# Linear attention and an MLP on one core: first turns of a group moved ahead of the stores, two PSUM tiles moved to other banks, one sum moved to VectorE

## The chip, the cores and the metric

The kernel runs on one NeuronCore of a Trainium2 chip. The time is the device time of one execution in microseconds; the median of three runs before the change is 224.44 us (221.71 to 224.67).

## The reference

For each of 4 batches and 8 heads, 768 tokens of width 64 go through a causal linear attention with a decay `lam` per head, and the result, 3072 tokens of 512 values, through an MLP of 512 to 2048 to 512 whose activation is Mish:

```python
for b in range(nb):                                   # blocks of 64 tokens
    intra = einsum('bhic,bhjc->bhij', qb, kb) * Dmask[None]
    intra = einsum('bhij,bhjd->bhid', intra, vb)
    inter = einsum('bhid,bhde->bhie', qb * lam_pow[None], kv_state)
    out[:, :, sl] = intra + inter
    kv_state = lam_block * kv_state + einsum('bhsd,bhse->bhde', kb * rev_pow[None], vb)
h = x @ w_in                                          # (3072, 512) x (512, 2048)
g = h * tanh(log1p(exp(h)))
result = g @ w_out                                    # (3072, 2048) x (2048, 512)
```

## The kernel before

**Groups and rounds.** The 768 tokens of a batch are cut into 6 chunks of 128 (`C`). Group n is chunk n of all four batches: 512 tokens, 4 chunks numbered i = 4n + b. The outer loop over n ("round n") runs the MLP of group n and, in between, the attention of group n + 1. A round is a list of units for TensorE (PE): 16 units of the first layer (`mm1_unit`: 4 matmuls of 128x512 into a bank `ph`, then Mish on ScalarE into `hsg`), then for n >= 1 fourteen halves of the second layer (`fast_unit`: 7 products x, z, x, z, y, z, y for 2 token blocks, 8 matmuls of 128x256 each). The seven products are a Strassen-like scheme: `token_sum` makes sums `gsum` of Mish outputs on VectorE (DVE), and `after` combines the products (`p1`, `p7`, `u3`, `u2`, `osum`) and stores four quarters.

**Attention of groups 2 to 5** comes in pieces, of which `room` says how many are done after which unit. `chunk_a` forms k^T v (`pv`), adds the old state (`raw`, DVE), multiplies by the decay (`w`, GpSimd, which is POOL in the profile), and turns chunk b + 2. `chunk_s` forms the scores `pS` from the transposed k and q and masks them (`sb`, DVE). `chunk_o` forms the output `pO`, scales it (`xtok`, DVE) and transposes it by DMA into `xt`, which the first layer of the next round reads. The 12 pieces of a group stand as a, s, a, s, o, a, s, o, a, s, o, o. Groups 0 and 1 have other pieces (`first_*`, `att_*`).

**A turn** (`turn(i)`) scales k by its decay into `ktil` (POOL; DVE for the last group), then issues two DMA transposes on SP's queue: `qraw` from q and `kraw` from `ktil`. The scores of chunk i need both. The first two turns of a group were made at unit 0 of the round, the other two in `chunk_a` of chunks 0 and 1.

**Queues.** The order within each engine is the order in which the code is written. SP issues the transposes of `turn`, those of `xtok`, and the stores of `after` at steps 4, 5 and 6 (units 25, 27, 29); each waits for its source, and what stands behind it waits as well. POOL issues the loads of k, q and v (`later`: 12 for the group after next, spread over a round) between its own arithmetic.

**PSUM** has 8 banks: `ph` 2, `po` 2 (products x, z, y and unit 2 of the first layer), `pS`, `pk`, `pq` and `pO` one each. A tile whose name takes a bank waits until the readers of the tile before in that bank are done.

Of the kernel before, what the change touches and what calls it, by code (L numbers as in the profile page):

```python
# [7 lines left out]
F32 = mybir.dt.float32  # L8
# [12 lines left out]
def kernel(  # L21
# [10 lines left out]
    nc = tc.nc  # L32
    B, H, S, D = q.shape
    C = 128
    NG = S // C
    JP = H // 2
# [231 lines left out]
    def turn(i):  # L268

        scale_k(i)  # L270
        for src, name, to in ((qn, "qraw", qraw), (ktil, "kraw", kraw)):
            to[i] = work.tile([128, JP, C], F16, name=name, tag=name, bufs=4)
            nc.sync.dma_start_transpose(out=to[i], in_=src[i].rearrange("p h c -> p (h c)"))
# [103 lines left out]
    def chunk_a(s):  # L377

        n, b = s.n, s.b
        i = n * B + b  # L380
        if n < NG - 1:
            pv = ps.tile([128, JP, 128], F32, name="pv", tag="pq")
            for j in range(JP):
                nc.tensor.matmul(  # L384
                    pv[:, j, :].rearrange("p (a e) -> p a e", a=2),
                    ktil[i][:, 2 * j : 2 * j + 2, :].rearrange("p h c -> p (h c)"),
                    vz[i % NVB][:, 2 * j : 2 * j + 2, 0:D], start=True, stop=True,
                )
            for hf in range(2):
                raw = work.tile([128, 2, 128], F32, name="raw", tag="raw", bufs=3)  # L390
                hs = slice(2 * hf, 2 * hf + 2)
                nc.vector.tensor_tensor(  # L392
                    out=raw, in0=pv[:, hs, :], in1=wst[b][hf][n % 2], op=ALU.add)
                nc.gpsimd.tensor_tensor(  # L394
                    out=wst[b][hf][(n + 1) % 2], in0=raw, in1=lbm[:, hs, :], op=ALU.mult)
        if i + 2 < (n + 1) * B:
            turn(i + 2)
# [15 lines left out]
    def chunk_o(s):  # L413

        n, b = s.n, s.b
        i = n * B + b
        if xt[n] is None:
            xt[n] = work.tile([128, JP, GT], F16, name="xt", tag="xt", bufs=2)
        psO = ps.tile([128, H, D], F32, name="pO", tag="pO")
        for j in range(JP):  # L420
            nc.tensor.matmul(  # L421
                psO[:, 2 * j : 2 * j + 2, :].rearrange("p h e -> p (h e)"), qraw[i][:, j, :],
                wst[b][j // 2][n % 2][:, j % 2, :], start=True, stop=False)
            for t in range(2):
                nc.tensor.matmul(psO[:, 2 * j + t, :], s.sb[t][:, j, :],  # L425
                                 vz[i % NVB][:, 2 * j + t, 0:D], start=False, stop=(t == 1))
        xtok = work.tile([128, H, D], F16, name="xtok", tag="xtok", bufs=4)
        nc.vector.tensor_tensor(out=xtok, in0=psO, in1=bc(lqt, 2, D), op=ALU.mult)  # L428
        nc.sync.dma_start_transpose(
            out=xt[n][:, :, b * C : (b + 1) * C], in_=xtok.rearrange("p h e -> p (h e)"))  # L430
# [196 lines left out]
    def after(n, step):  # L627

        if step == 0:
            nc.scalar.activation(keep(n, "p1"), bank[n, "x", "all"], AF.Copy)  # L630
        elif step == 1:
            nc.scalar.activation(keep(n, "p7"), bank[n, "z", "all"], AF.Copy)
        elif step == 2:
            o = work.tile([128, 2, HN], F32, name="osum", tag="osb", bufs=4)
            nc.scalar.activation(o, bank[n, "x", "all"], AF.Copy)
            store(n, 0, 0, o, nc.scalar)
        elif step == 3:
            nc.vector.tensor_tensor(  # L638
                out=keep(n, "u3"), in0=bank[n, "z", "all"], in1=kept[n, "p1"], op=ALU.add)
            nc.gpsimd.tensor_tensor(  # L640
                out=keep(n, "u2"), in0=kept[n, "u3"], in1=kept[n, "p7"], op=ALU.subtract)
        elif step == 4 and n < NG - 1:
            plus(n, 1, 1, "y", kept[n, "u3"])
        elif step == 4:
            o = work.tile([128, 2, HN], F32, name="osum", tag="osb", bufs=4)
            for t, b, lo, w in bank[n, "y"]:
                nc.vector.tensor_tensor(out=o[:, b, lo : lo + w], in0=t,
                                        in1=kept[n, "u3"][:, b, lo : lo + w], op=ALU.add)
            store(n, 1, 1, o, nc.sync)
        elif step == 5:  # L650
            plus(n, 1, 0, "z", kept[n, "p1"])
        elif step == 6:
            plus(n, 0, 1, "y", kept[n, "u2"])
# [53 lines left out]
    for n in range(NG):  # L707
        units = [(mm1_unit, (n, ni)) for ni in range(NKI)]

        if n == 0:  # L710
            units += [(mm2_unit, (n, b2 + b, part)) for b2 in range(0, B, 2) for part in range(WS)
                      for b in range(2)]
        else:
            units += [(fast_unit, (n, step, blk)) for step in range(7) for blk in range(2)]
        pieces = []
        if n + 1 < NG:
            pieces = att_pieces(n + 1) if n + 1 < NT else chunk_pieces(n + 1)
        if n == 0:

            i = max(i for i, (f2, _) in enumerate(pieces) if f2 is att_a)  # L720
            pieces[i : i + 3] = pieces[i + 1 : i + 3] + pieces[i : i + 1]

        if n == 0:
            room = dict(zip(range(24, 32), (1, 2, 3, 3, 3, 3, 3, 3)))
        else:
            first = 8 if n == 1 else 5
            span = len(units) - 8 - first
            room = {first + u: (u + 1) * len(pieces) // span - u * len(pieces) // span
                    for u in range(span)}
        if n == 1:  # L730

            for ni in range(3):
                mm1_part(n, ni, 0, GT - C)
                while late and ni < 2:
                    f2, s = late.pop(0)
                    f2(s)
                    if f2 is att_o:
                        break
        later = []
        if 1 <= n < NG - 2:  # L740
            later = [(lambda f=f, i=i: f(i)) for i in range((n + 2) * B, (n + 3) * B)
                     for f in (load_k, load_q, load_v)]
        nl = len(later)
        for u, (fn, args) in enumerate(units):
            rest = fn(*args)
            while later and (nl - len(later)) * len(units) <= u * nl:
                later.pop(0)()
            if n == 0 and 19 <= u < 23:
                weight_sum(0 if u < 21 else 2, u % 2)
            if n == 1 and 4 <= u < 8:  # L750
                weight_sum(1 if u < 6 else 3, u % 2)
            if n > 0 and u in (9, 10):
                token_sum(n, 2, u - 9)
            if n > 0 and u == NKI - 3:
                token_sum(n, 0, 0)
            if n > 0 and u == NKI - 2:
                token_sum(n, 1, 0)
            if n > 0 and u == NKI - 1:
                token_sum(n, 0, 1)
                token_sum(n, 1, 1)  # L760
            if n > 0 and u in (NKI + 2, NKI + 3):
                token_sum(n, 3, u - NKI - 2)
            if n == 0 and 2 <= u < 2 + nh:
                att_kv(first_halves[u - 2], "po")
                att_w(first_halves[u - 2])
            if n == 0 and u % 2 == 1 and 0 < (u + 1) // 2 < B:
                scale_k((u + 1) // 2)
            if n == 0 and nh + 2 <= u < nh + 2 + NVB - B:
                nc.vector.memset(vz[u - nh - 2 + B][:, :, D : 2 * D], 0.0)
            if n == 0 and nh + 2 <= u < nh + 2 + NKB:  # L770
                nc.vector.memset(kz[u - nh - 2], 0.0)
            if n == 0 and u == 17:
                q_decays()
            if n == 0 and u == 16:
                nc.vector.tensor_scalar(out=maskT, in0=rel, scalar1=0.0, scalar2=None, op0=ALU.is_ge)
            if n == 0 and u == 18:
                scale_k(B)
            if n > 0 and pieces and u == 0:
                if n > 1:
                    turn((n + 1) * B)  # L780
                turn((n + 1) * B + 1)
            for _ in range(room.get(u, 0)):
                f2, s = pieces.pop(0)
                s.spare = "po" if u < NKI - 1 else "ph"
                f2(s)
            if n == 0 and rest:
                rest()
        if n == 0:
            late = pieces
            while ahead:  # L790
                ahead.pop(0)()
# [30 lines left out]
```

## Time and profile before

| | |
|---|---|
| profiled execution | 222.32 us |
| span of its instructions | 220.3 us |
| granted TensorE clock, mean | 0.991 |
| PE busy | 200.6 us (91%) |
| DVE busy | 123.0 us (56%) |
| POOL busy | 116.3 us (53%) |
| ACT busy | 90.3 us (41%) |
| moved by DMA | 26.75 MB, mean 121 GB/s |
| DMA transposes on SP | 48, median landing 3.1 to 4.3 us |

Busy time is the time in which an engine had an instruction running; PEld, the weight load, runs beside PE. An engine's idle time matters where the work that ends last waits for it. In the timelines a row gives start, time, engine, line, operation and out<-in; the brackets at the end hold the idle time of the engine before it and what ended that. Names in brackets such as kraw(10) mean the tile of chunk 10; in the rows the numbers are left out.

### The profile page before, as it was taken

Reading aid. Unit: us, or ns where it says so; the run is one execution under the profiler, and the core shown is the slowest. Engines: PE = TensorE matmul, PEld = TensorE weight load, DVE = VectorE, ACT = ScalarE, POOL = GpSimd, SP = SyncE. Lnnn points to the kernel's source line nnn. Section 1 sums busy time; section 2 is a strip of 40 time slices with the busy share of each in tenths; the row PEclk is TensorE's granted clock in tenths of the full one; section 3 lists DMA queues with packets and bytes.
Section 4 is the critical chain, followed back from the end, with each engine's and each line's share of the span. In section 5 each row is a group of like instructions: output and inputs, shape, how many; then the busy total and the mean of one; then the engine's idle time right before and its main releaser. Section 6 shows DMA issues by size and latency. Waiting matters only on the chain.

```text
span 220.3 us, 4222 instructions
## 1 busy us (share of the span) xinstructions
PE 200.6 (91%) x1672; PEld 129.0 (59%) x1672; DVE 123.0 (56%) x229; ACT 90.3 (41%) x159; POOL 116.3 (53%) x140
## 2 busy tenths in 40 slices
PE   7899999999993996996998993998999999999993
PEld 2465544676541686743587741576854587744893
DVE  6658653777543895315986302897345865313433
ACT  5565566667651321163431061532046531176410
POOL 7996335998999643956961955765600001100020
PEclk9999999999998899999999999999999999999999
DMA  9999999998999988899899799299596313310014
GB/s 128 149 153 201 205 205 169 182 136 125 147 145 149 135 74 119 115 195 132 88 94 143 95 188 164 35 122 88 122 191 128 71 27 95 107 39 0 1 54 140
DMA packets 112469, 26.75 MB, mean 121 GB/s; under 512 B 102594, under 2 KB 111938, under 8 KB 112450
## 3 DMA queue, kind: packets, MB, share of 16 engines
q0 software_dynamic: 78080, 13.37, 83.6%
q1 hardware_dynamic: 31392, 10.49, 25.0%
q10 hardware_dynamic: 2978, 2.62, 3.9%
q8 instruction: 13, 0.21, 0.4%
q14 instruction: 6, 0.05, 0.1%
HBM read 27.26 MB, written 6.29 MB: 152 GB/s over the span
## 4 chain that ended last, share of the span: by engine, by line
PE 71%; DMA 11%; DVE 8%; POOL 4%; issue 3%; SPq 1%; ACT 1%; ACTq 0%; DVEq 0%
PE ph L482 28%; PE z L587 12%; DMA kraw<-ktil 9%; PE y L587 6%; PE po L504 6%; PE x L587 5%; DVE gsum L560 2%; PE pS L406 2%; DVE sb L411 2%; DMA qn<-in_q_dram 2%; POOL kn L69 2%; PE fin L587 2%; PE pO L421 2%; PE pO L425 1%; PE pO L249 1%
## 5 line engine op out<-in xcount | busy, mean ns | idle before, releaser
L482 PE MATMUL ph<-xt,win 128*128 128x512 f16 (+2 forms) x404 | 90.5, 371 | 0.4 <-ACT hsg L496 0.2
L496 ACT ACTIVATE hsg<-ph 128x512 f16<-128x512 f32 x96 | 57.0, 597 | 79.0 <-PE ph L482 78.9
L482 PEld LDWEIGHTS <-win 128*128 128x128 f16 x404 | 36.8, 98 | 37.3 <-issue 1.4
L640 POOL TENSOR_TENSOR u<-u,p 128x512 f32<-128x512 f32 x5 | 6.3, 1263 | 63.8 <-DVE u L638 63.8
L587 PEld LDWEIGHTS <-gsum 128*128 128x128 f16 x336 | 31.2, 98 | 3.3
L394 POOL TENSOR_TENSOR w<-raw,lbm 128x256 f16<-128x256 f32 x24 | 19.2, 817 | 19.4 <-DVE raw L392 19.3
L411 DVE TENSOR_TENSOR sb<-pS,maskT 128x512 f16<-128x512 f32 x32 | 20.5, 680 | 13.9 <-PE pS L406 13.9
L587 PEld LDWEIGHTS <-hsg 128*128 128x128 f16 x240 | 22.6, 98 | 4.0
L69 POOL DMA_DIRECT2D kn<-in_k_dram x23 | 21.2, 923 | 4.7 <-DMA wout<-in_moe_w_out_dram 1.7
L77 POOL DMA_DIRECT2D qn<-in_q_dram x23 | 21.0, 913 | 4.8 <-DMA wout<-in_moe_w_out_dram 3.3
L560 DVE TENSOR_TENSOR gsum<-hsg 128x1024 f16<-128x1024 f16 x20 | 15.7, 785 | 13.5 <-ACT hsg L496 13.5
L80 POOL DMA_DIRECT2D vz<-in_v_dram x24 | 21.6, 903 | 3.0 <-DMA wout<-in_moe_w_out_dram 1.7
L587 PE MATMUL x<-wout,hsg 128*128 128x256 f16 x160 | 20.5, 273 | 0.0
L587 PE MATMUL z<-tsum,gsum 128*128 128x256 f16 x160 | 19.3, 273 | 0.0
L392 DVE TENSOR_TENSOR raw<-pv,w 128x256 f32<-128x256 f32 x24 | 9.1, 416 | 16.1 <-PE pv L384 15.5
L264 POOL TENSOR_TENSOR ktil<-kn,lk 128x512 f16<-128x512 f16 x15 | 15.8, 1063 | 0.1
L504 PE MATMUL po<-wout,hsg 128*128 128x512 f16 x64 | 15.1, 379 | 0.0
L406 PE MATMUL pS<-qraw,kraw 64*128 64x128 f16 x128 | 6.6, 224 | 8.7 <-DMA kraw<-ktil 8.7
L428 DVE TENSOR_TENSOR xtok<-pO,lqt 128x512 f16<-128x512 f32 x16 | 11.0, 685 | 5.1 <-PE pO L425 5.1
L421 PE MATMUL pO<-w,qraw 128*128 128x128 f16 x64 | 9.2, 223 | 4.0 <-DVE xtok L428 4.0
L406 PEld LDWEIGHTS <-kraw 64*128 64x128 f16 x128 | 3.7, 96 | 14.7 <-DMA kraw<-ktil 10.2
L425 PEld LDWEIGHTS <-sb 128*128 128x128 f16 x128 | 8.2, 100 | 4.7 <-issue 4.3
(101 smaller groups left out, 236.7 us busy)
## 6 DMA issues: line engine op xcount, KB each, us to landing
out_dram<-osum SPq DMA_DIRECT2D x14, 256.0 KB, 3.3
vz<-in_v_dram POOLq DMA_DIRECT2D x24, 128.0 KB, 5.5
kn<-in_k_dram POOLq DMA_DIRECT2D x23, 128.0 KB, 4.9
qn<-in_q_dram POOLq DMA_DIRECT2D x23, 128.0 KB, 4.8
wout<-in_moe_w_out_dram POOLq DMA_DIRECT2D x4, 512.0 KB, 16.1
win<-in_moe_w_in_dram POOLq DMA_DIRECT2D x3, 512.0 KB, 9.7
out_dram<-osum ACTq DMA_DIRECT2D x5, 256.0 KB, 3.0
out_dram<-osb ACTq DMA_DIRECT2D x4, 256.0 KB, 5.3
```

Source lines behind the costliest of these rows:

```text
L69: nc.gpsimd.dma_start(out=kn[i], in_=chunk_rows(k, i))
L77: nc.gpsimd.dma_start(out=qn[i], in_=chunk_rows(q, i))
L80: nc.gpsimd.dma_start(out=vz[i % NVB][:, :, 0:D], in_=chunk_rows(v, i))
L264: (nc.vector if i <= B or i >= (NG - 1) * B else nc.gpsimd).tensor_tensor(out=t, in0=kn[i], in1=bc(lk, 2, D), op=ALU.mult)
L394: nc.gpsimd.tensor_tensor(out=wst[b][hf][(n + 1) % 2], in0=raw, in1=lbm[:, hs, :], op=ALU.mult)
L406: nc.tensor.matmul(pS[t][:, j, :], kraw[i][rs, j, :], qraw[i][rs, j, :], start=True, stop=True)
L411: nc.vector.tensor_tensor(out=s.sb[t], in0=pS[t], in1=bc(maskT, 1, JP), op=ALU.mult)
L482: nc.tensor.matmul(ph_t[ni][:, lo:hi], win0[min(ni, 2)][:, kc, max(ni - 2, 0) * 128 : max(ni - 2, 0) * 128 + 128] if ni < w else win[ni // ...
L496: nc.scalar.activation(hsg[n][:, ni, :], ph_t.pop(ni), AF.Mish)
L504: nc.tensor.matmul(po, hsg[n][:, ki, b * C : (b + 1) * C], wout[part][:, kk, :], start=(ki == 0), stop=(ki == NKI - 1),)
L560: nc.vector.tensor_tensor(out=gsum[n, i][:, ks, :], in0=a, in1=b, op=op)
L587: nc.tensor.matmul(t, lhs(kk, b), rhs(kk, c, c + w), start=(fresh and kk == 0 and (alone or i == 0)), stop=(kk == HK - 1), skip_group_chec ...
```

## The change

Four things are named in its title, and the diff shows two more.

- For groups 3, 4 and 5 the first two turns are made after units 23 and 25 of the round before, and no longer at unit 0. Group 2 keeps its second turn at unit 0 of round 1.
- `pv` of the chunks takes a bank of `po` (up to unit 14) or of `ph` (from unit 15 on), and `pO` takes the banks `pO` and `pq` in turn.
- `u2 = u3 - p7` runs on DVE and no longer on POOL.
- In rounds 2 to 4 each attention piece comes two units earlier (`first` 3 where it was 5). Round 1 keeps its places.
- The 12 loads of a round start at unit 1 and end by unit 23, where they ran from unit 0 to unit 27.

```diff
-            pv = ps.tile([128, JP, 128], F32, name="pv", tag="pq")
+            pv = ps.tile([128, JP, 128], F32, name="pv", tag=s.spare, bufs=2)
...
-        psO = ps.tile([128, H, D], F32, name="pO", tag="pO")
+        psO = ps.tile([128, H, D], F32, name="pO", tag=("pO", "pq")[b % 2])
...
                 out=keep(n, "u3"), in0=bank[n, "z", "all"], in1=kept[n, "p1"], op=ALU.add)
-            nc.gpsimd.tensor_tensor(
+            nc.vector.tensor_tensor(
                 out=keep(n, "u2"), in0=kept[n, "u3"], in1=kept[n, "p7"], op=ALU.subtract)
...
-            first = 8 if n == 1 else 5
-            span = len(units) - 8 - first
+            first = 8 if n == 1 else 3
+            span = (22 if n == 1 else 20) - first
             room = {first + u: (u + 1) * len(pieces) // span - u * len(pieces) // span
                     for u in range(span)}
...
-            while later and (nl - len(later)) * len(units) <= u * nl:
+            while later and u >= 1 and (nl - len(later)) * 24 <= (u - 1) * nl:
                 later.pop(0)()
...
-            if n > 0 and pieces and u == 0:
-                if n > 1:
-                    turn((n + 1) * B)
+            if n == 1 and u == 0:
                 turn((n + 1) * B + 1)
+            if n > 0 and n + 2 < NG and u in (23, 25):
+                turn((n + 2) * B + (u - 23) // 2)
```

How this moves instructions shows at three places. On SP's queue at the end of round 1, from the last transposed output of group 2 on (`osum` rows are the stores of steps 4, 5 and 6); before:

```order
L429 DMA_TRANSPOSE xt_1107<-xtok_1300 128x4x128
L615 DMA out_0_dram<-osum_1342 128x2x256
L615 DMA out_0_dram<-osum_1363 128x2x256
L615 DMA out_0_dram<-osum_1383 128x2x256
L273 DMA_TRANSPOSE qraw_1397<-qn_968 128x4x128
L273 DMA_TRANSPOSE kraw_1399<-ktil_1395 128x4x128
L273 DMA_TRANSPOSE qraw_1403<-qn_1038 128x4x128
L273 DMA_TRANSPOSE kraw_1405<-ktil_1401 128x4x128
```

and now:

```order
L429 DMA_TRANSPOSE xt_1109<-xtok_1304 128x4x128
L273 DMA_TRANSPOSE qraw_1330<-qn_968 128x4x128
L273 DMA_TRANSPOSE kraw_1332<-ktil_1328 128x4x128
L615 DMA out_0_dram<-osum_1351 128x2x256
L273 DMA_TRANSPOSE qraw_1356<-qn_1013 128x4x128
L273 DMA_TRANSPOSE kraw_1358<-ktil_1354 128x4x128
L615 DMA out_0_dram<-osum_1376 128x2x256
L615 DMA out_0_dram<-osum_1395 128x2x256
```

The first pair of transposes moved ahead of all three stores, the second pair ahead of two of them.

On POOL's queue at the start of round 1, from the last loads of group 2 to the scaling of chunk 10; before:

```order
L80 DMA vz_72<-in_v_dram 128x8x64
L69 DMA kn<-in_k_dram 128x8x64
L264 TENSOR_TENSOR ktil<-kn,lk 128x512
L77 DMA qn<-in_q_dram 128x8x64
L80 DMA vz_73<-in_v_dram 128x8x64
L69 DMA kn<-in_k_dram 128x8x64
L394 TENSOR_TENSOR w_187<-raw,lbm 128x256
L394 TENSOR_TENSOR w_189<-raw,lbm 128x256
L264 TENSOR_TENSOR ktil<-kn,lk 128x512
```

and now:

```order
L80 DMA vz_72<-in_v_dram 128x8x64
L264 TENSOR_TENSOR ktil<-kn,lk 128x512
L69 DMA kn<-in_k_dram 128x8x64
L77 DMA qn<-in_q_dram 128x8x64
L80 DMA vz_73<-in_v_dram 128x8x64
L69 DMA kn<-in_k_dram 128x8x64
L77 DMA qn<-in_q_dram 128x8x64
L394 TENSOR_TENSOR w_187<-raw,lbm 128x256
L394 TENSOR_TENSOR w_189<-raw,lbm 128x256
L264 TENSOR_TENSOR ktil<-kn,lk 128x512
```

The scaling of chunk 9 moved ahead of one load; one load more stands ahead of the multiplications of w and of the scaling of chunk 10.

On DVE in the second layer of round 2, from `raw` of the last chunk on (`u` is u3, and now u2 behind it); before:

```order
L392 TENSOR_TENSOR raw<-pv,w_199 128x256
L392 TENSOR_TENSOR raw<-pv,w_201 128x256
L560 TENSOR_TENSOR gsum_1677<-hsg,gsum_1594 128x1024 x2
L411 TENSOR_TENSOR sb<-pS,maskT 128x512 x2
L428 TENSOR_TENSOR xtok<-pO,lqt 128x512 x2
L638 TENSOR_TENSOR u_1772<-z,p_1653 128x512
L624 TENSOR_TENSOR osum<-y,u_1772 128x512
```

and now:

```order
L392 TENSOR_TENSOR raw<-pv,w_199 128x256
L392 TENSOR_TENSOR raw<-pv,w_201 128x256
L411 TENSOR_TENSOR sb<-pS,maskT 128x512 x2
L560 TENSOR_TENSOR gsum_1692<-hsg,gsum_1610 128x1024
L428 TENSOR_TENSOR xtok<-pO,lqt 128x512
L560 TENSOR_TENSOR gsum_1692<-hsg,gsum_1610 128x1024
L428 TENSOR_TENSOR xtok<-pO,lqt 128x512
L638 TENSOR_TENSOR u_1776<-z,p_1666 128x512
L640 TENSOR_TENSOR u_1778<-u_1776,p_1718 128x512
L624 TENSOR_TENSOR osum<-y,u_1776 128x512
```

The masked scores of the last chunk moved ahead of the last two token sums, and u2 stands between u3 and the first sum to be stored.

## The prediction

> **What bounds the kernel now.** I read the page's busy shares first, then busy time by round (one turn of the outer loop `n`), then the list of waits, the chain, and the timelines of PE, SP, POOL and DVE around each wait.
>
> ```profile
> PE 200.6 (91%) x1672; PEld 129.0 (59%) x1672; DVE 123.0 (56%) x229; ACT 90.3 (41%) x159; POOL 116.3 (53%) x140
> 57.00:91.94 34.94, 29.63 (x262) 19.99 (x261) 19.46 (x32) 10.76 (x19) 26.77 (x32) 0.95 1.55 123
> 91.94:125.45 33.51, 30.73 (x274) 20.49 (x272) 19.26 (x32) 11.34 (x19) 22.39 (x26) 1.00 1.31 126
> 125.45:160.58 35.13, 30.73 (x274) 20.52 (x272) 19.26 (x32) 11.34 (x19) 21.92 (x25) 1.00 1.21 121
> 160.58:190.91 30.33, 29.79 (x257) 19.56 (x256) 17.91 (x28) 11.34 (x19) 1.26 (x1) 1.00 0.57 99
> 190.91:217.00 26.09, 26.08 (x193) 17.34 (x190) 9.25 (x16) 11.34 (x19) 1.27 (x1) 1.00 0.13 41
> ```
>
> TensorE is the bound (columns: stretch, length, then busy time of PE, PEld, DVE, ACT, POOL, the granted clock). The five stretches are rounds 1 to 5, round 1 from its first full unit on. Rounds 2 and 3 hold the same 30.73 us of matmul but last 33.51 and 35.13; round 4 has 29.79 in 30.33; round 5, which carries no attention, has no hole. So what there is to win is the holes: 5.3, 2.8, 4.4 and 0.5 us in rounds 1 to 4. No other engine passes 27 us in such a stretch. The timeline of PE says what the holes are (in brackets the idle time before an instruction and what ended it):
>
> ```profile
> 70.34 0.61 PE L406 MATMUL pS<-qraw,kraw 64*128 64x128 f16 x8 [3.38 <-DMA kraw<-ktil]
> 84.34 0.22 PE L421 MATMUL pO<-w,qraw 128*128 128x128 f16 x1 [1.70 <-DVE xtok L428]
> 100.94 0.40 PE L406 MATMUL pS<-qraw,kraw 64*128 64x128 f16 x8 [1.87 <-DMA kraw<-ktil]
> 117.85 0.22 PE L421 MATMUL pO<-w,qraw 128*128 128x128 f16 x1 [0.90 <-DVE xtok L428]
> 136.07 0.40 PE L406 MATMUL pS<-qraw,kraw 64*128 64x128 f16 x8 [3.49 <-DMA kraw<-ktil]
> 152.98 0.22 PE L421 MATMUL pO<-w,qraw 128*128 128x128 f16 x1 [0.90 <-DVE xtok L428]
> 183.29 0.23 PE L421 MATMUL pO<-w,qraw 128*128 128x128 f16 x1 [0.54 <-DVE xtok L428]
> ```
>
> Two kinds only: scores `pS` that wait for the transposed k of a chunk (rounds 1, 2, 3), and the last output `pO` of a group that waits until `xtok` has read the single pO bank (rounds 1 to 4). The first kind is a queue matter:
>
> ```profile
> 92.75 0.37 SPq L615 DMA_DIRECT2D out_dram<-osum  x1
> 94.61 6.28 DMA kraw<-ktil
> 101.18 1.19 SPq L273 DMA_TRANSPOSE kraw<-ktil  x1
> 128.11 7.92 DMA kraw<-ktil
> kraw<-ktil SPq DMA_TRANSPOSE x1, 4.6
> DMA to landing us min/median/max: 2.4/4.2/5.9
> ```
>
> In round 2 the first kraw is issued at 94.61, after the third store (92.75), which itself waits for the last product of round 1. Four transposes and three loads are then in flight together, and kraw takes 6.28 us (7.92 in round 3), against a median landing of 4.2 for all of them; the one issued at 101.18 took 4.6.
>
> **The change, part by part.** Times are against the profiled execution, 222.32 us with a span of 220.3.
>
> *First turns moved to units 23 and 25 (rounds 1 to 3).* This moves two scalings on POOL (DVE for the last group) and four transposes on SP past three stores. POOL comes first: in rounds 2 and 3 the third multiplication of w, then the loads of units 15 to 23 (0.94 us each, row at 101.11 below) lie ahead of the scaling, and none of them waits for TensorE.
>
> ```profile
> L496 ACT ACTIVATE hsg<-ph 128x512 f16<-128x512 f32 x96 | 57.0, 597 | 79.0 <-PE ph L482 78.9
> L560 DVE TENSOR_TENSOR gsum<-hsg 128x1024 f16<-128x1024 f16 x20 | 15.7, 785 | 13.5 <-ACT hsg L496 13.5
> 74.53 0.86 PE ph L482 x4
> 75.39 0.87 PE x L587 x8
> ```
>
> Take P as the end of the last first-layer unit. Raw of chunk 3 ends at about P+2.9 (a Mish of 0.6, two token sums of 0.7 to 0.8 and raw itself, 0.76), its two multiplications at P+4.6, four loads at P+8.4, the two scalings of 1.0 at P+9.4 and P+10.5. On SP, the last xtok is done at P+7.4 (behind the z halves, two more token sums and another xtok), its transpose of 1.2 takes until P+8.7, qraw until P+9.9, so kraw(0) goes out at about P+10. The next round begins at P+13.7 (14 second-layer halves of 0.87 and the pieces of chunks 2 and 3 that fall there, 0.22 for a pv, 0.33 for a pS, 0.46 for each of two pO), and its first pS now stands behind unit 5, at 6 x 0.86 + 0.2 = 5.4 later: P+19.1. That leaves 9 us for a landing that took 7.92 at worst. kraw(1) goes after the first store (P+11), at P+12.8, and is due behind unit 8 at P+22.2. Both waits go: 1.87 + 3.49 = **5.4 us**. Queued behind these on SP are the stores, 1.3 us later at most (their buffers are used again 20 us on), and the third turn, which is not ready before.
>
> *Pieces two units earlier in rounds 2 to 4.* What is late next? The third kraw, which stays in its piece:
>
> ```profile
> 97.82 0.39 PE L384 MATMUL pv<-vz,ktil 128*128 128x128 f16 x4
> 108.76 0.40 PE L406 MATMUL pS<-qraw,kraw 64*128 64x128 f16 x8
> 98.25 0.76 DVE L392 TENSOR_TENSOR raw<-pv,w 128x256 f32<-128x256 f32 x2 [5.52 <-PE pv L384]
> 98.76 1.40 POOL L394 TENSOR_TENSOR w<-raw,lbm 128x256 f16<-128x256 f32 x2 [2.60 <-DVE raw L392]
> 101.11 0.94 POOL L69 DMA_DIRECT2D kn<-in_k_dram  x1
> ```
>
> From pv of chunk 0 (97.82) to pS of chunk 2 (108.76) are 10.94 us, 1.87 of them the hole: 9.07 without it. From pv to the issue of kraw(2) are 3.36 (101.18). So 5.7 us are left for a landing of 4.6: no wait, 1.1 to spare. I take 0, and the other end is 7.92 - 5.7 = 2.2 us in each of rounds 2 and 3.
>
> *k^T v on the first layer's spare banks, output on two banks.* The number of matmuls stays. pO of chunk 3 no longer shares a bank with chunk 2. In rounds 2 to 4 it now stands behind the whole second z half, at P+4.5, and its sb ends at P+4.2 (raw to P+2.9, then two in 1.27), so its wait goes entirely: 0.90 + 0.90 + 0.54 = **2.3 us**. In round 1 the pieces keep their places, and sb still bounds it:
>
> ```profile
> 82.42 1.27 DVE L411 TENSOR_TENSOR sb<-pS,maskT 128x512 f16<-128x512 f32 x2
> 83.61 0.67 DVE L428 TENSOR_TENSOR xtok<-pO,lqt 128x512 f16<-128x512 f32 x1
> ```
>
> sb ends at 83.69 and xtok at 84.28, so the wait shrinks by **0.6 us**. The price of pv's new banks is a wait for their last reader; pv is read within 1.2 us (98.25 + 0.76 against 97.82), the next user of a bank stands at least one unit of 0.86 and usually ten units behind, so 0. If that cover were gone it is a rival below.
>
> *Round 1's loads and turn 9.* The scaling of chunk 9 now stands ahead of one load on POOL, and five loads, not three, lie between it and the next w:
>
> ```profile
> 62.34 0.95 POOL L69 DMA_DIRECT2D kn<-in_k_dram  x1
> 63.23 1.14 POOL L264 TENSOR_TENSOR ktil<-kn,lk 128x512 f16<-128x512 f16 x1
> 64.39 5.90 DMA kraw<-ktil
> 66.91 1.46 POOL L394 TENSOR_TENSOR w<-raw,lbm 128x256 f16<-128x256 f32 x2
> 69.38 1.19 SPq L273 DMA_TRANSPOSE kraw<-ktil  x1
> kraw<-ktil SPq DMA_TRANSPOSE x1, 4.7
> 70.95 1.82 PE ph L482 x4
> 76.20 0.40 PE L406 MATMUL pS<-qraw,kraw 64*128 64x128 f16 x8
> 70.00:75.00 5.00, 4.66 (x35) 2.56 (x36) 3.73 (x6) 1.19 (x2) 3.49 (x5) 0.69 1.96 142
> ```
>
> kraw(9) goes out 0.9 earlier and lands at 69.4; the hole falls from 3.38 to 2.5. But kraw(10) follows 62.34 + 1.1 + 5 x 0.93 + 1.46 + 1.1 = 70.6, 1.2 later than 69.38, and lands at 75.3, where its pS stood at 76.20: the gain of this stretch ends at **0.9 us**. That holds for either clock. After the hole of 3.38 the granted clock was 0.69 (70 to 75), after 1.87 and 3.49 it was 1.00 (rounds 2 and 3 above). If it stays full after 2.5, the matmuls behind it save about 1.4 us (the four matmuls at 70.95 took 1.82 where 0.86 is usual; the pS and pO beside them 0.5 longer), which the later kraw(10) takes back, unless it lands in the fastest 2.4. So 0.9, with 0 and 2.3 as ends.
>
> The Trainium skill (TensorE: Matmul & The Clock Gate, What's actually happening) says that the clock halves after an idle window of about 3.4 us, a free-running one. By that rule 2.5 us of idling cannot halve it, and with kraw(10) in time the sum would be 1.4 lower, 211.7; the trace agrees only in part, since 3.38 us lowered it and 3.49 did not.
>
> *u2 on DVE.* One addition of 0.69 us (the time of the sum below, of the same shape) falls into the gap of 0.99 us between u3 and the first osum; POOL loses one that nothing on the path waited for:
>
> ```profile
> 88.49 0.69 DVE L624 TENSOR_TENSOR osum<-y,u 128x512 f32<-128x512 f32 x1 [0.99 <-PE y L587]
> ```
>
> It costs 0. Without that gap the first osum and its store are 0.7 later; the next product into the same y bank is two halves of 0.87 away, so even then TensorE does not wait.
>
> **Sum.** 5.4 + 2.3 + 0.6 + 0.9 = 9.2 us: 222.32 - 9.2 = 213.1. The profiled run was 2.1 under the median of the three shown (224.44; 221.71 to 224.67), counted from which it would be 215.2. I take about the middle, **214.0**.
>
> **Rivals.**
> *The hole moves to the third kraw* (faster, but less). For it: the landings of 5.9 to 7.9 when loads run beside, and now two loads directly follow its scaling instead of one. Against: 4.6 measured at this place. Price 2 x 2.2: 218.4.
> *The transposes are bound by the DMA engines, not by their place in SP's queue*, so the change does not do what it says. For it: the landing times rise together. Against: kraw's turn falls into a stretch with no load. Then only the pO and u2 parts are left, 2.9 us: 221.5.
> *Slower: k^T v waits in the dense layer's banks.* If the banks rotate so that the product after pv needs the bank that raw reads, TensorE stands from the end of pv (98.04) to that of raw (99.01), 1 us for each of 12 chunks in rounds 1 to 3: 214.0 + 12 = 226.0. It decides where fewer than one product separates pv and the next user. Against: with two banks in turn, the order has at least one product between in each case that I counted; for it: raw can be queued behind token sums on DVE.
>
> **How the numbers follow.** Forecast 0.70, third kraw 0.14, DMA bound 0.09, banks 0.07. A change of under 2% can't be told from none here (220.0 to 228.9). Faster holds the first two, 0.84; same the third, 0.09; slower the last, 0.07. The range: below, the 2.3 of round 1 and the profiled run's offset (212.6 less the scatter), 210.5; above, the third kraw's case and a little, 219.5. That leaves out the DMA and bank cases and a few hundredths more. The likeliest case alone spans 211 to 217.
>
> **What would show it.** Right: rounds 2 and 3 last about 30.7 us each; no pS waits for kraw there; the first kraw of rounds 2 and 3 is issued before the round begins; no pO wait in rounds 2 to 4; one pS wait of about 2.5 us in round 1 and perhaps another of 1. Wrong: a pS wait behind unit 12 (third kraw), a wait of ph, x or pv for DVE's raw, or SP standing in front of a scaling with stores behind it.

## The result, and the profile after

The changed kernel takes 214.82 us (median of 4 runs, 213.68 to 216.23) against 224.56 (median of 4 runs, 221.71 to 228.83) for the kernel before beside it. One execution of a kernel can be some per cent longer than another at a lower granted clock (the kernel before: 222.58 us at 0.998, 229.20 at 0.968), so all ratios here leave out executions over 1.5% above the fastest, such as that of 228.83 us, and rows marked * in the table of experiments come from profiles of such executions. The ratio is 0.961, 95% interval 0.949 to 0.973. The profiled execution takes 213.99 us, 8.33 less than before, with a span of 211.8.

Busy time by round in the changed kernel (length, then PE, PEld, DVE, ACT, POOL, the granted clock, the share of the DMA engines and GB/s):

```profile
57.00:90.87 33.87, 28.56 (x260) 19.29 (x260) 21.75 (x34) 10.72 (x19) 29.97 (x34) 1.00 1.85 135
90.87:122.16 31.29, 30.67 (x273) 20.43 (x273) 20.47 (x33) 11.34 (x19) 20.80 (x24) 1.00 1.39 134
122.16:152.66 30.50, 30.50 (x272) 20.47 (x273) 20.83 (x35) 11.34 (x19) 16.98 (x20) 1.00 1.31 143
152.66:182.28 29.62, 29.62 (x259) 19.63 (x258) 17.38 (x27) 11.34 (x19) 0.00 (x0) 1.00 0.38 88
```

Rounds 2 and 3 last 31.29 and 30.50 us, where about 30.7 each was forecast; rounds 3 and 4 have no hole left. These are all the holes that the PE timeline brackets from round 1 on, beside 0.24 us at its start:

```profile
68.50 0.40 PE L406 MATMUL pS<-qraw,kraw 64*128 64x128 f16 x8 [1.58 <-DMA kraw<-ktil]
74.89 0.40 PE L406 MATMUL pS<-qraw,kraw 64*128 64x128 f16 x8 [1.74 <-DMA kraw<-ktil]
81.84 0.20 PE L425 MATMUL pO<-vz,sb 128*128 128x64 f16 x1 [0.45 <-DVE sb L411]
82.43 0.20 PE L425 MATMUL pO<-vz,sb 128*128 128x64 f16 x1 [0.40 <-DVE sb L411]
90.87 4.48 PE L482 MATMUL ph<-xt,win 128*128 128x512 f16 x20 [0.90 <-issue]
122.16 4.48 PE L482 MATMUL ph<-xt,win 128*128 128x512 f16 x20 [0.62 <-issue]
```

Round 1's scores still wait, now twice, for k of chunks 9 and 10. The last two rows are new: the first matmul of rounds 2 and 3 starts late, and the timeline names no releaser ("issue"). The first layer reads `xt`, so the last DMA transpose of `xtok` is the candidate. SP's issue, and the landing of the DMAs issued there; first the changed kernel, then the one before:

```profile
115.18 1.24 SPq L429 DMA_TRANSPOSE xt<-xtok  x1
xt<-xtok SPq DMA_TRANSPOSE x1, 6.9
```

```profile
119.22 1.19 SPq L429 DMA_TRANSPOSE xt<-xtok  x1
xt<-xtok SPq DMA_TRANSPOSE x1, 2.6
```

Issued at 115.18, landed 6.9 later at 122.07, and the matmul starts at 122.16. Before, the same transpose took 2.6 us and landed at 121.8, 3.5 ahead of the next round. At all 15 late first matmuls of this kernel and the runs below, the last xt landed 0.09 to 0.10 us before the matmul, so it is what they wait for.

The first kraw of rounds 2 and 3 is now issued before the round begins, as forecast:

```profile
87.03 1.22 SPq L273 DMA_TRANSPOSE kraw<-ktil  x1
118.83 1.22 SPq L273 DMA_TRANSPOSE kraw<-ktil  x1
```

### The profile page after: what moved, and what is told of

It reads as the page before. It is cut to its first block, busy times and chain, and to the rows that moved or that the text cites. A ratio compares the mean times of both kernels' runs of the same rounds, so it can differ in the third digit from the quotient of the medians.

```text
span 211.8 us, 4225 instructions
## 1 busy us (share of the span) xinstructions
PE 198.4 (94%) x1672; PEld 127.8 (60%) x1672; DVE 127.9 (60%) x234; ACT 90.2 (43%) x159; POOL 110.6 (52%) x135
## 4 chain that ended last, share of the span: by engine, by line
PE 75%; POOL 13%; DMA 6%; DVE 2%; issue 2%; POOLq 0%; DVEq 0%
PE ph L482 32%; PE z L587 13%; PE x L587 7%; PE y L587 7%; PE po L504 7%; DMA win<-in_moe_w_in_dram 4%; POOL kn L69 3%; POOL vz L80 3%; POOL qn L77 3%; DMA kraw<-ktil 2%; PE pS L406 2%; PE fin L587 2%; PE pO L425 2%; PE pO L421 1%; POOL ktil L264 1%
## 5 line engine op out<-in xcount | busy, mean ns | idle before, releaser
L482 PEld LDWEIGHTS <-win 128*128 128x128 f16 x404 | 36.3, 98 | 38.9 <-issue 2.7
L394 POOL TENSOR_TENSOR w<-raw,lbm 128x256 f16<-128x256 f32 x24 | 18.6, 798 | 21.7 <-DVE raw L392 21.6
L560 DVE TENSOR_TENSOR gsum<-hsg 128x1024 f16<-128x1024 f16 x20 | 18.0, 913 | 13.2 <-ACT hsg L496 13.2
L587 PEld LDWEIGHTS <-hsg 128*128 128x128 f16 x240 | 22.9, 98 | 3.4
L587 PE MATMUL x<-wout,hsg 128*128 128x256 f16 x160 | 19.4, 273 | 0.0
L264 POOL TENSOR_TENSOR ktil<-kn,lk 128x512 f16<-128x512 f16 x15 | 16.8, 1129 | 0.1
L560 DVE TENSOR_TENSOR gsum<-hsg,gsum 128x1024 f16<-128x1024 f16 x10 | 7.6, 764 | 5.2 <-PE z L587 5.2
L264 DVE TENSOR_TENSOR ktil<-kn,lk 128x512 f16<-128x512 f16 (+1 forms) x9 | 6.2, 684 | 6.8 <-DMA kn<-in_k_dram 6.7
L425 PE MATMUL pO<-vz,sb 128*128 128x64 f16 x128 | 9.2, 193 | 0.8 <-DVE sb L411 0.8
L587 PE MATMUL z<-tsum,hsg 128*128 128x256 f16 x80 | 9.5, 272 | 0.0
L504 PEld LDWEIGHTS <-hsg 128*128 128x128 f16 x64 | 5.9, 97 | 5.9
## 6 DMA issues: line engine op xcount, KB each, us to landing
vz<-in_v_dram POOLq DMA_DIRECT2D x24, 128.0 KB, 4.8
kn<-in_k_dram POOLq DMA_DIRECT2D x23, 128.0 KB, 5.1
qn<-in_q_dram POOLq DMA_DIRECT2D x23, 128.0 KB, 5.4
```

The source lines that it names most:

```text
L264: (nc.vector if i <= B or i >= (NG - 1) * B else nc.gpsimd).tensor_tensor(out=t, in0=kn[i], in1=bc(lk, 2, D), op=ALU.mult)
L394: nc.gpsimd.tensor_tensor(out=wst[b][hf][(n + 1) % 2], in0=raw, in1=lbm[:, hs, :], op=ALU.mult)
L425: nc.tensor.matmul(psO[:, 2 * j + t, :], s.sb[t][:, j, :], vz[i % NVB][:, 2 * j + t, 0:D], start=False, stop=(t == 1))
L482: nc.tensor.matmul(ph_t[ni][:, lo:hi], win0[min(ni, 2)][:, kc, max(ni - 2, 0) * 128 : max(ni - 2, 0) * 128 + 128] if ni < w else win[ni // ...
L504: nc.tensor.matmul(po, hsg[n][:, ki, b * C : (b + 1) * C], wout[part][:, kk, :], start=(ki == 0), stop=(ki == NKI - 1),)
L560: nc.vector.tensor_tensor(out=gsum[n, i][:, ks, :], in0=a, in1=b, op=op)
```

## The experiments

Each was timed beside the kernel before. The startup differs by up to 2 us from one profiled execution to the next, so the table gives the rounds, each from its first matmul to that of the next (round 1 from its second unit on). Of the rows marked * only the named holes and landings are used below.

| kernel | ratio to before (95%) | round 1 | round 2 | round 3 | round 4 |
|---|---|---|---|---|---|
| before | 1 | 35.34 | 33.51 | 35.13 | 30.33 |
| changed | 0.961 (0.949 to 0.973) | 34.48 | 31.29 | 30.50 | 29.61 |
| turns back | 0.954 (0.946 to 0.962) | 34.33 | 31.19 | 31.92 | 29.72 |
| turns alone* | 0.961 (0.948 to 0.973) | 36.30 | 32.21 | 32.19 | 30.33 |
| one output bank | 0.967 (0.958 to 0.976) | 34.14 | 32.06 | 32.07 | 31.25 |
| loads as before | 214.97 us, no interval | 34.17 | 31.08 | 30.80 | 29.61 |
| loads alone | 0.993 (0.984 to 1.002) | 34.14 | 33.69 | 34.33 | 30.33 |
| both back | 0.973 (0.958 to 0.989) | 36.41 | 32.13 | 32.22 | 30.10 |
| sum on POOL | 0.960 (0.944 to 0.976) | 33.46 | 30.51 | 30.51 | 29.61 |
| round 1 mended | 0.950 (0.929 to 0.970) | 31.44 | 31.27 | 31.56 | 29.61 |
| sum alone* | 0.991 (0.985 to 0.997) | 36.45 | 34.45 | 35.34 | 30.33 |
| three back* | 1.002 (0.996 to 1.009) | 35.21 | 35.91 | 38.05 | 31.03 |
| all mended | 0.940 (0.931 to 0.950) | 32.21 | 30.50 | 30.51 | 29.61 |
| places back | 0.964 (0.949 to 0.980) | 34.72 | 30.96 | 30.96 | 29.65 |

### Turns back, and turns alone

```diff
 turns back, against the changed kernel (turns alone is the reverse, against the kernel before)
-            if n == 1 and u == 0:
-                turn((n + 1) * B + 1)
-            if n > 0 and n + 2 < NG and u in (23, 25):
-                turn((n + 2) * B + (u - 23) // 2)
+            if n > 0 and pieces and u == 0:
+                if n > 1:
+                    turn((n + 1) * B)
+                turn((n + 1) * B + 1)
```

> The changed kernel with its first two turns of groups 3 to 5 put back to unit 0 of the next round; all else as changed. Theory (the gain of 5.4 us comes from SP's order): kraw(0) of rounds 2 and 3 goes out 2.7 us after the round begins and lands 6.3 to 7.9 later, at 9.0 to 10.6, while its pS now stands at 5.4: holes of 3.6 and 5.2 us, 8.8 in all, less the 0.9 and 0.6 us by which the first matmul of rounds 2 and 3 starts late: about 7 us more than the changed kernel, 221 to 222 us. Rival (the gain comes from the new pacing of loads, so that DMA transposes land fast wherever they are issued): landings near 4.2, holes of 1.5 or less each, 215 to 217 us.

> The kernel before with only the first two turns of groups 3 to 5 moved to units 23 and 25. Theory: the pS waits of rounds 2 and 3 go (1.87 and 3.49 us), the pO waits of 1.70, 0.90, 0.90, 0.54 and round 1's kraw wait of 3.4 stay: 5.4 us under the kernel before, ratio 0.976. If the late first matmul of rounds 2 and 3 comes from the turns' transposes beside the last xt, it shows here too, by up to 1 us each, and the ratio is 0.98 to 0.985. Rival (the pieces' places or the loads' pace made the gain): 1.00.

PE with the turns put back, round 3, and with the turns alone, rounds 2 and 3:

```profile
129.85 0.40 PE L406 MATMUL pS<-qraw,kraw 64*128 64x128 f16 x8 [0.81 <-DMA kraw<-ktil]
```

```profile
119.28 0.22 PE L421 MATMUL pO<-w,qraw 128*128 128x128 f16 x1 [1.55 <-DVE xtok L428]
151.47 0.22 PE L421 MATMUL pO<-w,qraw 128*128 128x128 f16 x1 [1.53 <-DVE xtok L428]
```

Taken alone, the new turns do remove the kraw waits of rounds 2 and 3, as forecast. The ratio, 0.961, is lower than the 0.976 worked out; part of that goes with the granted clock, 0.992 to 1.000 in the runs compared and 0.977 to 0.992 in those of the kernel before beside them. (The pO waits grew from 0.90 to 1.5: the pair of token sums ahead of the last masked scores took 2.25 us for 1.66, with POOL's w beside it. Why they met so is open.) But putting the turns back brings only one kraw wait of 0.81 us, not 8.8. The theory that SP's order alone made these waits has fallen: something else in the change removes them too. The time, 216.09 us, is the one that the rival named; whether its cause, the pace of the loads, holds is tested below.

### One output bank

```diff
-        psO = ps.tile([128, H, D], F32, name="pO", tag=("pO", "pq")[b % 2])
+        psO = ps.tile([128, H, D], F32, name="pO", tag="pO")
```

> The changed kernel with pO on its one bank again; pv stays on the dense layer's banks. Theory: the last pO of each group waits for xtok of chunk 2, which DVE now does behind a token sum: in round 2 it could start at 113.7 where it started at 112.3, so 1.3 us in each of rounds 2 to 4 and 0.4 in round 1, about 4.3 us more than the changed kernel: 218.5 to 219.5 us, more than the 2.3 + 0.6 that the bank was forecast to save. Rival (the pieces' earlier places had removed the pO wait already): no change, 214 to 215 us.

```profile
84.64 0.22 PE L421 MATMUL pO<-w,qraw 128*128 128x128 f16 x1 [1.69 <-DVE xtok L428]
115.01 0.23 PE L421 MATMUL pO<-w,qraw 128*128 128x128 f16 x1 [1.39 <-DVE xtok L428]
147.08 0.23 PE L421 MATMUL pO<-w,qraw 128*128 128x128 f16 x1 [1.39 <-DVE xtok L428]
178.34 0.22 PE L421 MATMUL pO<-w,qraw 128*128 128x128 f16 x1 [1.48 <-DVE xtok L428]
```

1.4 to 1.5 us in each of rounds 2 to 4, as worked out, and 0.8 more in round 1; 219.19 us. These waits add up to 5.1 us, but the late first matmuls of rounds 2 and 3 (0.90 and 0.62) are gone with the bank, so that by rounds 1 to 4 this kernel is 3.6 us longer than the changed one. With the pieces at their new places the second bank is worth that much, more than the 2.9 us that it was brought in for.

### Loads as before, and loads alone

```diff
 loads as before, against the changed kernel (loads alone is the reverse, against the kernel before)
-            while later and u >= 1 and (nl - len(later)) * 24 <= (u - 1) * nl:
+            while later and (nl - len(later)) * len(units) <= u * nl:
```

> The changed kernel with the 12 loads of a round paced as before (unit 0 to 27). Two theories of the late first matmul of rounds 2 and 3 (0.90 and 0.62 us, with the last xt landing 6.5 and 6.9 us after its issue). If the loads that now stand packed at units 19 to 23 slow it, the hole goes here: 1.5 us less. If the turns' transposes beside it slow it, the hole stays. In round 1, kraw(9)'s wait grows by about 0.9 (its scaling is again behind one load), kraw(10)'s 1.74 goes (its scaling is again behind one load fewer): 0 to 1 us less. Total 212.5 to 215 us.

> The kernel before with only the loads paced as in the change (unit 1 to 23). With the turns at unit 0 as changed, kraw(0) had landed within about 5 us and rounds 2 and 3 had lost little, so the order on SP is not the only thing that can remove these waits. Theory now (either suffices: turns ahead of the stores, or a start of the round without loads beside the transposes): kraw(0) goes out 2.7 us after the round begins and lands in 4.3 to 5, at 7 to 7.7, where its pS stands at 7.1: the holes of 1.87 and 3.49 shrink to under 0.7 each; rounds 2 and 3 last 31.8 to 32.5 us (33.5 and 35.1 before). Rival (the late pS waits are SP's order alone, and the run with turns put back was a lucky one): the holes stay at 1.5 to 3.5 us.

With the loads as before, PE's holes of round 1 and of round 3's start, and the clock behind the first (third number from the end):

```profile
69.25 0.49 PE L406 MATMUL pS<-qraw,kraw 64*128 64x128 f16 x8 [2.55 <-DMA kraw<-ktil]
121.43 4.48 PE L482 MATMUL ph<-xt,win 128*128 128x512 f16 x20 [0.41 <-issue]
70.00:75.00 5.00, 5.00 (x33) 2.88 (x32) 3.98 (x7) 1.52 (x3) 4.33 (x5) 0.72 1.46 137
```

Round 1 goes as expected: kraw(9) waits 0.97 longer, kraw(10) not at all. The late start of round 2 goes, that of round 3 shrinks to 0.41: the loads have a part in it. With the loads alone, the kraw waits of rounds 2 and 3 stay:

```profile
101.77 0.40 PE L406 MATMUL pS<-qraw,kraw 64*128 64x128 f16 x8 [2.05 <-DMA kraw<-ktil]
136.10 0.40 PE L406 MATMUL pS<-qraw,kraw 64*128 64x128 f16 x8 [2.69 <-DMA kraw<-ktil]
```

So the pace of the loads is not the second cure; the rival above and this theory have fallen as well.

### Both back

Both edits above are undone in the changed kernel; banks, places and u2 on DVE stay.

> The changed kernel with both the turns and the loads as before; banks, sum and the pieces' earlier places as changed. Theory now (either suffices): with neither, kraw(0) lands 9.0 to 10.6 us into rounds 2 and 3, its pS stands at 5.4: holes of 3.6 and 5.2 us, rounds 2 and 3 of 34.3 and 35.9 us; about 8 us over the changed kernel, 222 to 223 us. Rival (banks or places gave the gain of rounds 2 and 3): these rounds stay under 32.5.

PE in rounds 2 and 3:

```profile
94.55 4.48 PE L482 MATMUL ph<-xt,win 128*128 128x512 f16 x20 [0.57 <-issue]
126.68 4.48 PE L482 MATMUL ph<-xt,win 128*128 128x512 f16 x20 [1.46 <-issue]
132.98 0.40 PE L406 MATMUL pS<-qraw,kraw 64*128 64x128 f16 x8 [0.74 <-DMA kraw<-ktil]
```

No 3.6 and 5.2, but 0 and 0.74. The rounds stay under 32.5 us, which was the sign of the rival, banks or places; three back, below, keeps both and has the holes. POOL's queue around the end of round 1 shows what is left of the change. Before, then with both back (the round ends at 91.8 and 94.6):

```profile
87.59 1.26 POOL L640 TENSOR_TENSOR u<-u,p 128x512 f32<-128x512 f32 x1 [3.62 <-DVE u L638]
88.81 0.91 POOL L69 DMA_DIRECT2D kn<-in_k_dram  x1
...
92.34 2.08 POOL L264 TENSOR_TENSOR ktil<-kn,lk 128x512 f16<-128x512 f16 x2
```

```profile
86.67 0.88 POOL L69 DMA_DIRECT2D kn<-in_k_dram  x1
...
90.16 2.09 POOL L264 TENSOR_TENSOR ktil<-kn,lk 128x512 f16<-128x512 f16 x2
```

Before, u2 stands in POOL's queue and waits 3.62 us for u3; four loads and the two scalings behind it wait as well, then run into the first transposes of the next round. With u2 gone to DVE they are done earlier by 5 us relative to the end of the round. That makes u2, the term priced at nothing, the candidate for the second cure; the next three runs test it.

### Sum alone, three back, sum on POOL

```diff
 sum alone, against the kernel before (sum on POOL is the reverse, against the changed kernel;
 three back: the changed kernel with turns, loads and this sum undone)
-            nc.gpsimd.tensor_tensor(
+            nc.vector.tensor_tensor(
                 out=keep(n, "u2"), in0=kept[n, "u3"], in1=kept[n, "p7"], op=ALU.subtract)
```

> The kernel before with only u2 moved to DVE. The changed kernel without its new turns and loads had still no long kraw wait; what it kept was u2 on DVE. Theory now: on POOL u2 waits for u3, and the loads and the scalings of the first turns wait behind it, so that four loads are still in flight when the next round's transposes start; with u2 on DVE these loads go earlier, kraw(0) goes out 2.0 us into the round (2.8 before) and lands in 2.5 to 4.5, before its pS at 7.1. Rounds 2 and 3 lose their holes of 1.87 and 3.49 and last about 31.6 us each, up to 0.5 more where the last xt lands late: 4.5 to 5.4 us less, ratio 0.976 to 0.98. Rival (the pieces' places or pv's bank did it): rounds 2 and 3 stay at 33.5 and 35.

> The changed kernel with turns, loads and u2 all as before; only the banks and the pieces' earlier places as changed. Theory: with none of the two cures, kraw(0) goes out 2.8 us into rounds 2 and 3 and lands in 6.3 to 7.9, while its pS stands at 5.4: holes of 3.6 and 5.2 us, rounds 2 and 3 of 34 to 36 us, 4 to 8 us over the changed kernel. Rival (the earlier places or banks cure it): rounds 2 and 3 at 30.5 to 32.5.

> The changed kernel with u2 back on POOL. Theory: nobody on the path waits for it on either engine; 0, within 0.5 us of the changed kernel by its rounds. Rival (POOL's queue counts: u2 waits for u3 there, with the loads and the scalings of the turns behind it): kraw(0) and kraw(1) of rounds 2 and 3 go out 2 to 5 us later, at the end of the round, which their slack of 4 us just covers or misses by 1: up to 2 us more.

Three back, PE in rounds 2 and 3, has the holes as worked out, 3.65 and 5.09, and gains nothing as a whole:

```profile
102.49 0.40 PE L406 MATMUL pS<-qraw,kraw 64*128 64x128 f16 x8 [3.65 <-DMA kraw<-ktil]
139.83 0.61 PE L406 MATMUL pS<-qraw,kraw 64*128 64x128 f16 x8 [5.09 <-DMA kraw<-ktil]
```

It differs from both back in the engine of u2 alone, so it is u2 on DVE that took these waits away there. Without turns and u2 the longer kraw holes (8.74 us for 5.36, and one of 1.35 in round 4) cost about what the banks bring. Sum alone has no kraw wait in rounds 2 to 4, which the theory asked for, but late first matmuls in their place (SP's and the DMA rows: the last xt of round 2):

```profile
93.70 6.20 PE L482 MATMUL ph<-xt,win 128*128 128x512 f16 x28 [0.42 <-issue]
128.16 7.89 PE L482 MATMUL ph<-xt,win 128*128 128x512 f16 x28 [2.00 <-issue]
163.49 7.07 PE L482 MATMUL ph<-xt,win 128*128 128x512 f16 x32 [1.21 <-issue]
120.03 1.52 SPq L429 DMA_TRANSPOSE xt<-xtok  x1
xt<-xtok SPq DMA_TRANSPOSE x1, 8.0
```

120.03 + 8.0 = 128.0, and the matmul starts at 128.16. There are no new turns here; what the edit moves beside this xt are loads: POOL issues six from 116.10 to 121.43, where before it issued none between 116.61 and 122.31. The landings of all runs agree: from 90 us on, the transposes on SP whose landing the traces tell took 2.4 us in the median where they overlapped no load, and 5.1 where they overlapped four (a landing that is long for another reason also meets more loads, so this is no proof by itself). The pO waits grew as well, to 1.63 and 1.61, and of the expected 2% sum alone keeps 0.9%. Sum on POOL is the counterpart: turns ahead of the stores, u2 holding back the loads, and rounds 2 and 3 without a hole:

```profile
89.90:120.41 30.51, 30.51 (x275) 20.52 (x272) 19.53 (x32) 11.34 (x19) 22.03 (x27) 1.00 1.44 139
120.41:150.91 30.50, 30.50 (x274) 20.51 (x272) 20.72 (x34) 11.34 (x19) 20.36 (x24) 1.00 1.44 143
```

The forecast delay of kraw did come, and its slack covered it. By its rounds 1 to 4 this kernel is 1.8 us shorter than the changed one; the runs (212.31 to 215.82 against 213.68 to 216.23 us) do not resolve that.

### Round 1 mended, and all mended

```diff
 round 1 mended, against the changed kernel (in all mended: 16 for 20, u2 on POOL, and rounds 2 and 3 paced as changed)
             while ahead:
                 ahead.pop(0)()
+                if len(ahead) == 3:
+                    turn(2 * B + 1)
...
-            if n == 1 and u == 0:
-                turn((n + 1) * B + 1)
...
-            while later and u >= 1 and (nl - len(later)) * 24 <= (u - 1) * nl:
+            while later and (
+                    u >= 10 and (nl - len(later)) * 20 <= (u - 10) * nl if n == 1
+                    else (nl - len(later)) * len(units) <= u * nl):
```

> The changed kernel with three edits: turn(9) is made after the sixth of the nine loads that stand ahead of it on POOL at the start of round 1, the loads of round 1 begin at unit 10 only, and those of rounds 2 and 3 are paced as before. Theory (round 1's two kraw waits are POOL's queue: load issues of 0.9 us each ahead of the scalings): kraw(9) goes out 2.5 us earlier, at about 61, kraw(10) at about 67 and not 70.2, both waits (1.58 and 1.74) go, round 1 lasts 31.0 to 31.6 us (34.5 as changed), and the whole 211 to 212 us against 214 to 215. Rival (these transposes are late because the DMA engines are full at this point): the landings lengthen by what the issue gains, and round 1 stays above 33.5.

> The changed kernel with u2 back on POOL (rounds 2 and 3 then lasted 30.5 us each) and round 1 mended: turn(9) inside the row of loads, the loads of round 1 from unit 10 on. Theory: rounds 1 to 3 of 31.0 to 31.6, 30.5 and 30.5 us, the span 207 to 208.5 us with a start as in the changed kernel's profile, 209.5 to 211 us in the profiled execution. Rival (round 1's loads, pressed into units 10 to 26, now collide with the last xt and the first turns of round 2): round 1 ends with a hole of 0.5 to 1 us before the first matmul of round 2, or round 2 has a kraw wait of that size.

PE in round 1 of all mended:

```profile
78.44 0.21 PE L406 MATMUL pS<-qraw,kraw 64*128 64x128 f16 x1 [1.24 <-DVE sb L411]
79.03 0.38 PE L406 MATMUL pS<-qraw,kraw 64*128 64x128 f16 x7 [0.39 <-DVE sb L411]
82.59 0.20 PE L425 MATMUL pO<-vz,sb 128*128 128x64 f16 x1 [0.81 <-DVE sb L411]
83.19 0.20 PE L425 MATMUL pO<-vz,sb 128*128 128x64 f16 x1 [0.39 <-DVE sb L411]
```

Both kraw waits of round 1 go, in both kernels: counted from the second unit, kraw(9) is issued 2.2 to 2.3 us earlier than in the changed kernel and still lands in 4.6 to 5.5 us (5.0 there). So they were POOL's row of load issues, not the DMA engines. DVE's sb is the next to wait for, so round 1 falls to 31.4 in round 1 mended, as worked out, and to 32.2 in all mended, above its forecast of 31.0 to 31.6. Round 1 mended as a whole missed its 211 to 212 us (213.34): the first matmuls of rounds 3 and 4 are late there by 0.30 and 0.89. All mended is the fastest version: 210.97 us, 0.940 (0.931 to 0.950) of the time before, with rounds 2 to 4 at 30.5, 30.5 and 29.6.

### Places back

```diff
-            first = 8 if n == 1 else 3
-            span = (22 if n == 1 else 20) - first
+            first = 8 if n == 1 else 5
+            span = len(units) - 8 - first
```

> The changed kernel with the pieces of rounds 2 to 4 back at their old units (first 5); turns, loads, banks and u2 as changed. Theory of the pO wait: two banks alone do not remove it, since at the old units the masked scores sb of the last chunk stand behind two token sums on DVE; pO then waits for sb as it still does in round 1 of the changed kernel (0.45 + 0.40 there, and 0.3 to 0.9 here) in each of rounds 2 to 4: 1 to 2.5 us more than the changed kernel. The last xt is issued two units later, about 1.7 us nearer to the end of the round, so the late first matmul of rounds 2 and 3 (0.90, 0.62) grows by up to 1.7 each if the landing stays at 6.5. Together 217 to 219 us. Rival (the banks alone remove the wait, the places do nothing): 214 to 215.5 us, no bracketed pO wait in rounds 2 to 4.

```profile
91.10 6.20 PE L482 MATMUL ph<-xt,win 128*128 128x512 f16 x28 [0.92 <-issue]
114.69 0.20 PE L425 MATMUL pO<-vz,sb 128*128 128x64 f16 x1 [0.28 <-DVE sb L411]
```

The hole of 0.92 is the end of round 1, whose places the edit leaves alone. In rounds 2 and 3 pO waits for sb, 0.28 us in each, as the theory asked for but less. Their late first matmul did not grow: in place of 0.62 there is none at the end of round 2, since the last xt, issued later, landed in 5.1 us for 6.9. Together rounds 2 and 3 are within 0.2 us of the changed kernel, and 215.39 us is the rival's time, though its sign, no pO wait, is not: next to two banks the earlier places do nothing that can be measured. My theory of the late xt was too simple: its landing does not only depend on its place in the round.

## Why the prediction was right, and where not

The forecast of 214.0 us was met (214.82), by a sum that was 0.87 us too high: two terms came out larger by 0.65 in all, and a wait that it did not see took 1.52. That these nearly cancel is luck. Against the profiled execution before, by the brackets of the PE timeline:

| term | forecast | measured |
|---|---|---|
| kraw waits of rounds 2 and 3 | 5.4 | 5.36 |
| pO waits of rounds 2 to 4 | 2.3 | 2.34 |
| pO wait of round 1 | 0.6 | 0.85 (1.70 to 0.45 + 0.40) |
| kraw(9) and kraw(10) in round 1 | 0.9 | 1.3 (pS of chunk 10 at 74.89 for 76.20) |
| first matmul of rounds 2 and 3 | not seen | -0.90 - 0.62 |
| sum | 9.2 | 8.33 |

That the sum meets the difference of the two profiled executions to the hundredth is chance: by the lengths of rounds 1 to 4 the gain is 0.86 + 2.22 + 4.63 + 0.72 = 8.43. A bracket is not the whole price of a wait: in round 1 the time from pS of chunk 10 to the z product behind the last pO fell by 0.67 us, where the brackets of pO give 0.85.

**First turns.** The waits went, but the step named one cause where there were two. kraw(0) was late since it stood behind the stores, and since u2 kept four loads back until they ran beside it. Either cure is enough: turns alone and sum alone both have no kraw wait in rounds 2 and 3, three back has 3.65 and 5.09. So 5.4 us is the joint gain of two edits, and the turns by themselves, within this change, are worth little: putting them back makes rounds 1 to 4 longer by 1.3 us. That the size came out is luck in part, since either edit would have given it. The second rival, the DMA engines, was half right as well: against it the prediction said that kraw's turn falls into a stretch with no load, but kraw(0) took 5.6 and 6.3 us to land, and only its earlier issue hid that. It went out at 118.83 in round 2, where P + 10 was 117.7.

**u2 on DVE** is the step that failed. It was costed by its own 0.69 us and by who waits for it; what stands behind it in POOL's queue was not counted. Alone it removes the kraw waits, and it lets the loads run into the last xt, whose landing rises from 2.6 us to 8.0. With the turns moved as well, only that price is left: the last xt of rounds 1 and 2 lands in 6.5 and 6.9 us, where it takes 4.9 and 5.9 with u2 on POOL, and the rounds are 1.0 and 0.8 us longer. This is the wait that the sum did not see.

**Third kraw.** Named as what is late next, with 1.1 us to spare; no pS behind unit 12 waits, and the rival with 218.4 us did not come.

**Banks.** No row of PE waits for DVE's raw: the slow rival did not come. What the second output bank is worth was undersized: 2.9 us were forecast, taking it away again costs 3.6 by the rounds, because the new places put xtok of chunk 2 behind a token sum.

**Round 1.** The second wait, for kraw(10), came as worked out (issued at 70.24 for 70.6, landed at 74.84 for 75.3). The clock stayed at 1.00 behind a hole that was shorter than forecast, 1.58 us for 2.5, since kraw(9) landed in 5.0 us and not 5.9. The two holes together are as long as the one before (1.58 + 1.74 for 3.38); the 1.3 us are the matmuls behind the first, which run at the full clock, and the prediction said that they would save 1.4 and that a later kraw(10) would take much of it back. What the clock does behind 2.5 us it left open; the run with the loads as before has 0.72 behind 2.55.

## What to carry to other kernels

An instruction that waits for another engine holds back everything behind it in its own queue; moving it to another engine is priced by that queue (here four loads and two scalings), not by its own duration. Where a wait has two late parents, undoing one cure shows little: each must be tried alone and both taken away together before a gain is given to an edit. Loads that are released earlier are not free either: what lands last in the stretch they move into gets later (here 6.9 us for 5.9, and 8.0 for 2.6 where the sum moved alone).

## What the runs showed of the hardware that I had not expected

*The clock behind a short hole.* The granted clock of the following 5 us was 0.72 behind a hole of 2.55 us and 0.69 behind 3.38, but 1.00 behind 3.49 and 1.58. The Trainium skill (TensorE: Matmul & The Clock Gate, What's actually happening) gives about 3.4 us for the idle window; by these rows a hole shorter than that can lower the clock as well, and the length alone does not decide. In sum alone it was 0.66 behind 2.00 us. The clock records show what else does. Between startup and end each lowered stretch lasts 3.41 us or twice that, and within one execution they begin whole steps of 3.41 us apart: in three back, 73.16, 103.88 and 138.01 are 9 and 10 steps apart. Counted so from the lowered stretch of the kernel before (69.70 to 73.11), a step ends at about 134.5, in the middle of the hole of 3.49 us (132.58 to 136.07). The holes of 2.55 and 2.00 us each lie within the step that ends where their clock drops (69.42 and 129.47). How much idling within a step lowers the clock is not shown.

*DVE beside POOL.* In the changed kernel the first u2 on DVE took 1.47 us, and the other four took 0.69 each, as every u3 of the same shape, which reads one input from PSUM. The first stands beside the scaling of k on POOL; the u3 ahead of it, also beside a scaling, was not slowed. One token sum, which reads two inputs from SBUF, took 1.78 us beside a scaling:

```profile
84.83 0.69 DVE L638 TENSOR_TENSOR u<-z,p 128x512 f32<-128x512 f32 x1 [1.12 <-PE z L587]
85.56 1.47 DVE L640 TENSOR_TENSOR u<-u,p 128x512 f32<-128x512 f32 x1
84.41 2.07 POOL L264 TENSOR_TENSOR ktil<-kn,lk 128x512 f16<-128x512 f16 x2
73.14 1.78 DVE L560 TENSOR_TENSOR gsum<-hsg 128x1024 f16<-128x1024 f16 x1
73.09 1.03 POOL L264 TENSOR_TENSOR ktil<-kn,lk 128x512 f16<-128x512 f16 x1
```

The Trainium skill (SBUF — State Buffer, Who interferes with whom) says that a DVE instruction with two SBUF inputs contends with a GpSimd instruction that reads SBUF; these rows agree: 1.47 us for u2 and 1.78 for a token sum, each 0.7 where POOL is idle. The u3 beside a scaling, with one SBUF input, kept its 0.69.
